# GpSimd takes over the scaling and clamping of the first six weight units, and the opening of a fused attention and feed-forward kernel is put in a new order

## The chip, the cores and the metric

The kernel runs on one core of a Trainium2 chip. The core's engines have their own instruction queues, and each works through its queue strictly in order: TensorE (PE; its weight loads are listed as PEld), VectorE (DVE), ScalarE (ACT), GpSimd (POOL) and SyncE (SP), which here only issues transfers. The metric is the device time of one execution in microseconds; the median of three runs counts.

## The reference

Attention within chunks of 64 tokens, then a feed-forward block with an ELU between two products:

```python
scores = scale * np.matmul(q_c, k_c.transpose(0, 1, 2, 4, 3))   # chunks of 64 tokens, head_dim 64
scores = scores - np.max(scores, axis=-1, keepdims=True)
attn = np.exp(scores)
attn = attn / (np.sum(attn, axis=-1, keepdims=True) + 1e-09)
out = np.matmul(attn, v_c)                                      # 8 batches, 8 heads, 576 tokens
...
h = x @ w_in                                                    # x: 4608 x 512, w_in: 512 x 2048
g = np.where(h > 0.0, h, alpha * (np.exp(np.minimum(h, 0.0)) - 1.0))
return (g @ w_out).astype(np.float32)                           # w_out: 2048 x 512
```

q, k and v arrive as 32-bit floats, the two weight matrices as 64-bit floats.

## The kernel before

**Blocks and products.** The 4608 tokens are nine blocks of 512, and a block is four tiles of 128 tokens. Every matrix product runs on numbers split into a high and a low part (`xhi`, `xlo`; `wi_hi`, `wi_lo`; `wo_hi`, `wo_lo`; `ghi`, `glo`), and is the sum of three products, high by high, high by low and low by high. In block one, `hidden(f)` makes 128 rows of the hidden layer (tile `h`) from all four tiles of x in 12 matrix products of 128x512, `elu` turns them into `e`, `ghi` and `glo`, and `second_products` adds four times three products with `w_out` to the outputs `o`. f runs from 0 to 15. Below, H0 is `hidden(0)` and S0 the second products for f = 0.

**Weights come in units.** Unit u holds 128 columns of `w_in` (rows of the hidden layer u) and 128 rows of `w_out` (for f = u - 1), as pairs of 32-bit words; unit 0 has only the first. `load_unit` loads a unit into one of three buffers `st`. `prepare_units` has two steps for each unit, both on ScalarE: the high words are multiplied by `REBIAS` (L139), and the low words are brought to a form that can be joined (L144). `merge_units` then has on VectorE a clamp of the high words (L161) and two joins that build a 32-bit float in `xf` (L168, L172); ScalarE casts that to `wi_hi` and `wo_hi` (L179). `subtract_next` makes `wi_lo` and `wo_lo` on VectorE (L185). A unit's operations on high words are 128x1024, those of unit 0 are 128x512. A buffer `st` is free for the unit after next but one when L172 has read it.

**Start.** Before block one, four tiles go through `early_attention`, in ten steps: turn q and k (PE, L270), copy them (ACT, L277), scores (PE, L248), maximum and difference (DVE, L283 to L299), exponential (ACT, L303, or eight small ones, L293, for a tile in `BY_HEAD`), sum, reciprocal and product of the probabilities (DVE, L305 to L308), turn the probabilities (PE, L315), copy (ACT, L322), times v (PE, L256), and split into `xhi` (ACT, L425) and `xlo` (DVE, L426). H0 needs `xhi` of all four tiles.

**What sets the order.** Two strings of tokens are executed one after another, and each token appends instructions to the engines' queues. In `START`, q, k, v and u with a number issue loads, a single digit is the next step of that tile, r the next step of `prepare_units`, d the next step of `merge_units`, and s a `subtract_next`. `FIRST_BLOCK` has the same letters, and H for `hidden`, e for the next of four steps of `elu`, P for second products, L4 to L7 for the loads of block two's tiles, and 4 to 7 for their next step.

Of the kernel before, what the change touches and what calls it, by code (L numbers as in the profile page):

```python
# [10 lines left out]
F32 = mybir.dt.float32  # L11
# [4 lines left out]
ALU = mybir.AluOpType  # L16
# [4 lines left out]
def kernel(  # L21
# [19 lines left out]
    nc = tc.nc  # L41

    B, H, S, D = q.shape
# [4 lines left out]
    P = 128  # L48
# [4 lines left out]
    NK = DM // P  # L53
# [4 lines left out]
    NS = (NB - PLAIN) // 2  # L58
    NG = NF // 2
    LAG = 1  # L60
    T2 = TB - P

    REBIAS = 2.0 ** -112
    LARGEST = float(np.uint32(0x0FEFFFFF).view(np.float32))
# [8 lines left out]
    at = ctx.enter_context(tc.tile_pool(name="at", bufs=1))  # L73
# [6 lines left out]
    xhi = const.tile([P, NK, TB], F32R, name="xhi")  # L80
    xlo = const.tile([P, NK, TB], F32R, name="xlo")
# [50 lines left out]
    def prepare_units():  # L132

        for u in range(NU):
            low, high, _ = units[u]

            nc.scalar.mul(out=high.bitcast(F32), in_=high.bitcast(F32), mul=REBIAS)  # L139
            prepared.add((u, "high"))  # L140
            yield

            top = low.bitcast(U16)[:, :, :, :, 1]
            nc.scalar.activation(  # L144
                out=low, in_=top, func=AF.Copy, scale=2.0 ** -13, bias=2.0 ** -14 - 0.5
            )
            prepared.add((u, "low"))
            yield

    def merge_units():  # L150


        def need(u: int, word: str):
            while (u, word) not in prepared:
                next(preparation)

        for u in range(NU):
            low, high, parts = units[u]
            highf = high.bitcast(F32)
            need(u, "high")  # L160
            nc.vector.tensor_scalar(  # L161
                out=highf, in0=highf, scalar1=LARGEST, scalar2=-LARGEST, op0=ALU.min, op1=ALU.max
            )
            yield
            need(u, "low")
            y = ybuf[u % 2].bitcast(U32).rearrange(
                "p (i a t) -> p i a t", i=2, a=4)[:, :len(parts)]
            nc.vector.scalar_tensor_tensor(  # L168
                out=y, in0=high, scalar=3, in1=low, op0=ALU.logical_shift_left, op1=ALU.bitwise_or
            )  # L170
            yield
            nc.vector.scalar_tensor_tensor(  # L172
                out=y, in0=high, scalar=0x80000000, in1=y, op0=ALU.bitwise_and, op1=ALU.bitwise_or
            )
            for i, (hi, _) in enumerate(parts):
                w = y[:, i].bitcast(F32)
                if len(hi.shape) > len(w.shape):
                    w = w.rearrange("p b (c d) -> p b c d", d=Q)
                nc.scalar.copy(out=hi, in_=w)  # L179
                merged.append((parts[i], w))  # L180
            yield
# [79 lines left out]
    def first_halves(pair_of_banks):  # L261
        return pair_of_banks[:, :, :NK * C].rearrange("p i (h t) -> p i h t", h=NK)

    def early_attention(tt: int, q_sb, k_sb, get_v, kT, at, a_pool, get_banks, put, by_head: bool):


        both = get_banks()
        for i, src in enumerate((q_sb, k_sb)):
            for hp in range(NK):
                nc.tensor.transpose(  # L270
                    out=both[:, i, hp * P:(hp + 1) * P], in_=src[:, 2 * hp:2 * hp + 2, :],
                    identity=ident,
                )
        yield
        qT = at.tile([P, NK, P], F32, name="qT")
        for i, to in enumerate((qT, kT)):
            nc.scalar.copy(out=to, in_=both[:, i, :].rearrange("p (h t) -> p h t", h=NK))  # L277
        yield
        scores = first_halves(both)
        score(scores, qT, kT)  # L280
        yield
        mx = sm.tile([P, 2, NK, 1], F32, name="mx")
        nc.vector.tensor_reduce(out=mx, in_=scores, axis=AX.X, op=ALU.max)  # L283
        a = a_pool.tile([P, H, C], F32, name="a")
        a_heads = a.rearrange("p (j h) t -> p j h t", j=2)
        z = sm.tile([P, 2, NK, 1], F32, name="z")
        if by_head:

            nc.vector.tensor_scalar_mul(mx, mx, -SCALE)
            yield  # L290
            for j in range(2):
                for h in range(NK):
                    nc.scalar.activation(  # L293
                        out=a_heads[:, j, h, :], in_=scores[:, j, h, :], func=AF.Exp, scale=SCALE,
                        bias=mx[:, j, h, :], accum_out=z[:, j, h, :],
                    )
            yield
        else:
            nc.vector.tensor_tensor(  # L299
                out=a_heads, in0=scores, in1=mx.broadcast_to([P, 2, NK, C]), op=ALU.subtract  # L300
            )
            yield
            nc.scalar.activation(out=a, in_=a, func=AF.Exp, scale=SCALE)  # L303
            yield
            nc.vector.tensor_reduce(out=z, in_=a_heads, axis=AX.X, op=ALU.add)  # L305
        nc.vector.tensor_scalar_add(z, z, 1e-9)
        nc.vector.reciprocal(z, z)
        nc.vector.tensor_tensor(  # L308
            out=a_heads, in0=a_heads, in1=z.broadcast_to([P, 2, NK, C]), op=ALU.mult
        )  # L310
        yield
        turned_ps = both[:, 0, :].rearrange("p (h t) -> p h t", h=H)
        for h in range(H):
            for half in halves:
                nc.tensor.matmul(  # L315
                    turned_ps[half, h, :], lhsT=a[half, h, :], rhs=ident[half, half],
                    start=True, stop=True,
                )
        yield

        aT = at.tile([P, NK, P], F32, name="qT").rearrange("p h (j t) -> p (h j) t", j=2)
        nc.scalar.copy(out=aT, in_=turned_ps)  # L322
        yield
        x_ps = first_halves(both)
        multiply_v(x_ps, get_v(), aT.rearrange("p h (u t) -> p u h t", u=2))
        yield
        put(tt, x_ps)
        yield
# [111 lines left out]
    def hidden(f: int):  # L440
        hi, lo = w_in_slices(f)
        h = ps_h.tile([P, TB], F32, name="h")
        if f:
            for kt in range(NK):
                three(h, hi[:, kt, :], lo[:, kt, :], xhi[:, kt, :], xlo[:, kt, :],
                      kt == 0, kt == NK - 1)
        else:
            terms = [(w, xhi, kt) for w in (hi, lo) for kt in range(NK)]
            terms += [(hi, xlo, kt) for kt in range(NK)]
            for i, (w, x, kt) in enumerate(terms):  # L450
                nc.tensor.matmul(h, lhsT=w[:, kt, :], rhs=x[:, kt, :], start=i == 0,  # L451
                                 stop=i == len(terms) - 1)
        return h
# [564 lines left out]
    def warm(n: int):  # L1018
# [7 lines left out]

    BY_HEAD = (2, 4, 5)
    START = (
        "q0 k0 q1 k1 w13 v0 0 1 0 q2 0 k2 q3 0 k3 1 1 v1 0 2 v2 1 3 0 2 2 v3 1 2 3 u0 3 1 2 u1 0 "
        "r r 1 3 1 0 3 2 2 d u2 d 1 0 r d 3 3 2 s 2 0 r d 1 d 3 r 2 3 3"  # L1030
    )
    FIRST_BLOCK = (
# [7 lines left out]
    )  # L1040
    SECOND_BLOCK = (
# [83 lines left out]
    w0 = ctx.enter_context(tc.tile_pool(name="w0", bufs=1))  # L1125
    weights.append((*w_in_tiles(w0), *w_out_tiles(w0)))
    with (
        tc.tile_pool(name="start", bufs=NTT) as start,
        tc.tile_pool(name="ps_start", bufs=NTT, space=bass.MemoryType.PSUM) as ps_start,
    ):  # L1130
# [6 lines left out]
        def start_step(item: str):  # L1137
            tt = int(item)
            if tt not in tiles:
                tiles[tt] = early_attention(  # L1140
                    tt, *[loaded[kind, tt] for kind in "qk"], lambda: loaded["v", tt],
                    start.tile([P, NK, P], F32, name="kT"), start, start,
                    lambda: start_banks() if tt else warmed[0],
                    split_first_x, tt in BY_HEAD)
            next(tiles[tt])

        for item in START.split():
# [64 lines left out]
    run, f, early_tiles = (0, o_tiles(), None), -1, {}  # L1212
# [732 lines left out]
```

## Time and profile before

| | |
|---|---|
| median of three runs | 825.47 us (822.76 to 828.17) |
| the profiled execution, its own time | 825.15 us |
| its span | 823.4 us |
| PE busy | 804.4 us, 98% of the span |
| DVE busy | 613.1 us, 74% |
| ACT busy | 523.5 us, 64% |
| POOL busy | 171.1 us, 21% |

All rows of a profile below are of that one execution: start in microseconds from the start of the span, duration, engine, line of the kernel, operation, output and inputs, and in brackets the idle time before it and what ended it. Durations overlap a little, since an engine starts the next instruction before the last one has fully drained.

### The profile page before, as it was taken

How to read it: one execution, taken by the hardware profiler on the slowest of the kernel's cores; microseconds unless marked ns; L12 is line 12 of the kernel's file. 1: busy time of each engine (PE TensorE's matmuls, PEld its weight loads, DVE VectorE, ACT ScalarE, POOL GpSimd, SP SyncE). 2: the span in 40 equal slices, each digit the busy share in tenths (PEclk: the TensorE clock that was granted, in tenths of full speed). 3: DMA queues.
4: the chain of work that ended last, by engine and by line, in shares of the span. 5: the costliest groups of instructions: out<-in, count | busy, mean ns of one | idle time of the engine just before them, and what ended most of it. 6: DMA issues, size and time to landing. Idle time of an engine off the chain costs nothing.

```text
span 823.4 us, 15851 instructions
## 1 busy us (share of the span) xinstructions
PE 804.4 (98%) x5853; PEld 655.6 (80%) x5853; DVE 613.1 (74%) x914; ACT 523.5 (64%) x990; POOL 171.1 (21%) x149
## 2 busy tenths in 40 slices
PE   6799999999999999999999999999999999999997
PEld 5688878888778878878888888778788888888885
DVE  4999997666776659767656867868889956557964
ACT  5999885544554546766666445888867737776451
POOL 0000014264525531443111254000020100000100
PEclk9999999999999999999999999999999999999999
DMA  9976994889778887689986789999876585566755
GB/s 234 272 212 209 270 328 130 244 243 267 219 215 231 231 269 205 202 241 281 283 235 188 218 246 299 286 322 287 249 204 206 195 269 193 193 196 190 226 186 149
DMA packets 183229, 191.90 MB, mean 233 GB/s; under 512 B 84720, under 2 KB 151792, under 8 KB 183152
## 3 DMA queue, kind: packets, MB, share of 16 engines
q1 hardware_dynamic: 182512, 188.80, 77.2%
q0 software_dynamic: 640, 2.10, 0.6%
q8 instruction: 46, 0.75, 0.4%
q14 instruction: 31, 0.25, 0.1%
HBM read 144.18 MB, written 42.99 MB: 227 GB/s over the span
## 4 chain that ended last, share of the span: by engine, by line
PE 83%; DMA 8%; SPq 3%; ACT 2%; DVE 2%; issue 1%; DVEq 0%; ACTq 0%
PE o L434 43%; PE h L434 34%; DMA ring<-a_dram 3%; PE ps_a L248 2%; PE ps_a L256 2%; SPq L206 2%; PE h L451 1%; DMA st<-in_moe_w_out_dram 1%; DMA kept<-in_k_dram 1%; DMA a_dram<-wi_lo 1%; DMA kept<-in_q_dram 1%; DMA a_dram<-wi_hi 1%; DMA v_sb<-in_v_dram 1%; PE ps_a L315 1%; DMA ring<-w_dram 1%
## 5 line engine op out<-in xcount | busy, mean ns | idle before, releaser
L434 PE MATMUL o<-wo_hi,ghi 128*128 128x512 f32 x272 | 107.6, 396 | 0.0
L434 PE MATMUL o<-wo_hi,glo 128*128 128x512 f32 x272 | 106.1, 390 | 0.3 <-DVE glo L479 0.3
L434 PE MATMUL o<-wo_lo,ghi 128*128 128x512 f32 x272 | 106.0, 390 | 0.0
L434 PE MATMUL h<-xhi,wi_hi 128*128 128x512 f32 x228 | 84.0, 397 | 0.1
L434 PE MATMUL h<-xlo,wi_hi 128*128 128x512 f32 x228 | 82.3, 390 | 0.0
L434 PE MATMUL h<-xhi,wi_lo 128*128 128x512 f32 x180 | 70.3, 390 | 0.0
L434 PEld LDWEIGHTS o<-wo_hi,glo 128*128 128x128 f32 x272 | 51.1, 188 | 11.7 <-DVE glo L479 0.7
L434 PEld LDWEIGHTS o<-wo_hi,ghi 128*128 128x128 f32 x272 | 51.0, 188 | 11.1
L434 PEld LDWEIGHTS o<-wo_lo,ghi 128*128 128x128 f32 x272 | 51.1, 188 | 10.2
L510 POOL TENSOR_TENSOR kept<-wi_hi,wi_lo 128x512 f32<-128x512 f32 x16 | 21.7, 1376 | 158.8 <-DVE xf L172 118.2
L471 DVE SCALAR_TENSOR_TENSOR e<-e,h 128x512 f32<-128x512 f32 x48 | 32.8, 684 | 25.2 <-ACT e L469 24.8
L434 PE MATMUL o<-split,ring 128*128 128x512 f32 x216 | 51.0, 390 | 0.0
L434 PEld LDWEIGHTS h<-xhi,wi_hi 128*128 128x128 f32 x228 | 42.6, 188 | 9.8 <-ACT kept L785 0.8
L434 PEld LDWEIGHTS h<-xlo,wi_hi 128*128 128x128 f32 x228 | 42.8, 188 | 8.5
L434 PEld LDWEIGHTS o<-split,ring 128*128 128x128 f32 x216 | 40.5, 188 | 8.4
L393 ACT COPY unturned<-turned 128x512 f32<-128x512 f32 x28 | 17.4, 621 | 46.0 <-DVE turned L388 37.9
L468 ACT ACTIVATE e<-h 128x512 f32<-128x512 f32 x48 | 28.6, 596 | 25.0 <-PE h L434 22.5
L476 ACT CAST ghi<-e 128x512 fp32r<-128x512 f32 x48 | 29.8, 621 | 19.8 <-DVE e L471 19.6
L746 POOL TENSOR_TENSOR glo<-e,ghi 128x512 fp32r<-128x512 f32 x16 | 20.7, 1296 | 96.9 <-ACT ghi L744 96.9
L434 PE MATMUL h<-split,ring 128*128 128x512 f32 x168 | 40.3, 391 | 0.0
L1492 ACT ACTIVATE e<-e 128x512 f32<-128x512 f32 x64 | 39.5, 630 | 1.0
L434 PEld LDWEIGHTS h<-xhi,wi_lo 128*128 128x128 f32 x180 | 33.8, 188 | 7.5 <-DVE wi_lo L185 0.4
(225 smaller groups left out, 2011.3 us busy)
## 6 DMA issues: line engine op xcount, KB each, us to landing
ring<-a_dram SPq DMA_DIRECT2D x56, 512.0 KB, 5.3
ring<-w_dram SPq DMA_DIRECT2D x56, 512.0 KB, 4.3
wi_hi<-a_dram SPq DMA_DIRECT2D x56, 256.0 KB, 5.3
kept<-in_q_dram SPq DMA_DIRECT2D x100, 128.0 KB, 3.8
kept<-in_k_dram SPq DMA_DIRECT2D x100, 128.0 KB, 4.0
wo_lo<-lo_dram SPq DMA_DIRECT2D x20, 512.0 KB, 5.8
v_sb<-in_v_dram SPq DMA_DIRECT2D x32, 256.0 KB, 5.4
st<-in_moe_w_in_dram SPq DMA_DIRECT2D x16, 512.0 KB, 4.9
```

What stands on the lines that cost most here:

```text
L206: nc.sync.dma_start(out=dst[p0:p0 + n], in_=src[b, :, s0:s0 + n, :].rearrange("h s d -> s h d"))
L248: nc.tensor.matmul(scores[halves[c], j, hp, :], lhsT=qT[halves[j], hp, halves[c]], rhs=kT[halves[j], hp, halves[c]], start=True, stop=True,)
L256: nc.tensor.matmul(x_ps[halves[j], c, hp, :], lhsT=v_sb[halves[c], 2 * hp + j, :], rhs=aT[halves[c], :, j * NK + hp], start=True, stop=True,)
L315: nc.tensor.matmul(turned_ps[half, h, :], lhsT=a[half, h, :], rhs=ident[half, half], start=True, stop=True,)
L393: nc.scalar.copy(out=unturned, in_=turned)
L434: nc.tensor.matmul(ps, lhsT=a, rhs=b, start=start, stop=stop, skip_group_check=onto)
L468: nc.scalar.activation(out=e, in_=h, func=AF.Relu, scale=-1.0)
L471: nc.vector.scalar_tensor_tensor(out=e, in0=e, scalar=-1.0, in1=h, op0=ALU.add, op1=ALU.max)
L476: nc.scalar.copy(out=ghi, in_=e)
L510: nc.gpsimd.tensor_tensor(out=out, in0=a, in1=b, op=op)
L746: engine.tensor_tensor(out=lo, in0=e, in1=hi.bitcast(F32), op=ALU.subtract)
L1492: nc.scalar.activation(out=units[u], in_=units[u], func=AF.Exp, scale=-1.0)
```

## The change

Four edits. For units 0 to 5 (`NPOOL = 6`), scaling and clamping of the high words leave ScalarE and VectorE, and two instructions on GpSimd take their place (multiply and minimum, then maximum). For tile 1 the product of the probabilities with the reciprocal sums moves from VectorE to GpSimd. `hidden` adds its terms for f up to 2 with the high weights first (high by high, high weights by low x, then low weights). And `START` and the beginning of `FIRST_BLOCK` are in a new order, with GpSimd's queue in the order of the program.

```diff
+    NPOOL = 6
...
-            nc.scalar.mul(out=high.bitcast(F32), in_=high.bitcast(F32), mul=REBIAS)
+            highf = high.bitcast(F32)
+            if u < NPOOL:
+                nc.gpsimd.tensor_scalar(
+                    out=highf, in0=highf, scalar1=REBIAS, scalar2=LARGEST, op0=ALU.mult, op1=ALU.min)
+                nc.gpsimd.tensor_scalar(
+                    out=highf, in0=highf, scalar1=-LARGEST, scalar2=None, op0=ALU.max)
+            else:
+                nc.scalar.mul(out=highf, in_=highf, mul=REBIAS)
...
-            nc.vector.tensor_scalar(
-                out=highf, in0=highf, scalar1=LARGEST, scalar2=-LARGEST, op0=ALU.min, op1=ALU.max
-            )
-            yield
+            if u >= NPOOL:
+                nc.vector.tensor_scalar(
+                    out=highf, in0=highf, scalar1=LARGEST, scalar2=-LARGEST, op0=ALU.min, op1=ALU.max
+                )
+            if u > 3:
+                yield
...
-        nc.vector.tensor_tensor(
+        (nc.gpsimd if normal_on_pool else nc.vector).tensor_tensor(
             out=a_heads, in0=a_heads, in1=z.broadcast_to([P, 2, NK, C]), op=ALU.mult
...
-        if f:
+        if f > 2:
...
-            terms = [(w, xhi, kt) for w in (hi, lo) for kt in range(NK)]
-            terms += [(hi, xlo, kt) for kt in range(NK)]
+            terms = [(hi, x, kt) for x in (xhi, xlo) for kt in range(NK)]
+            terms += [(lo, xhi, kt) for kt in range(NK)]
...
     START = (
-        "q0 k0 q1 k1 w13 v0 0 1 0 q2 0 k2 q3 0 k3 1 1 v1 0 2 v2 1 3 0 2 2 v3 1 2 3 u0 3 1 2 u1 0 "
...
+        "q0 k0 q1 k1 w13 v0 0 1 0 q2 0 k2 q3 0 k3 v1 1 1 0 1 2 v2 1 3 2 3 0 2 2 3 u0 u1 1 2 3 v3 0 "
...
```

**ScalarE's queue in the start**, from the exponentials of tile 2 (L293 before, L303 after) to the first operations of block one. `qT` written by L322 (L332 after) is the copy of the turned probabilities, `st` a weight unit. Before:

```order
L293 ACTIVATE a,z<-ps_a,mx 128x64 x8
L139 ACTIVATE st<-st 128x512
L144 ACTIVATE st<-st 128x512
L322 COPY qT<-ps_a 128x512 x2
L303 ACTIVATE a<-a 128x512
L139 ACTIVATE st<-st 128x1024
L179 CAST wi_hi<-xf 128x512
L322 COPY qT<-ps_a 128x512
L425 CAST xhi<-ps_a 128x2x4x64
L144 ACTIVATE st<-st 128x1024
L425 CAST xhi<-ps_a 128x2x4x64
L322 COPY qT<-ps_a 128x512
```

After:

```order
L303 ACTIVATE a,z<-ps_a,mx 128x64 x8
L332 COPY qT<-ps_a 128x512
L313 ACTIVATE a<-a 128x512
L149 ACTIVATE st<-st 128x512
L332 COPY qT<-ps_a 128x512 x2
L435 CAST xhi<-ps_a 128x2x4x64
L332 COPY qT<-ps_a 128x512
L435 CAST xhi<-ps_a 128x2x4x64 x2
L188 CAST wi_hi<-xf 128x512
L435 CAST xhi<-ps_a 128x2x4x64
L149 ACTIVATE st<-st 128x1024 x2
```

The scalings of units 0 to 2 (L139) are gone, tile 3's exponential stands ahead of unit 0's low words, and all four `xhi` stand ahead of the low words of units 1 and 2.

**GpSimd's queue after the identity matrix is made.** L318 is the product for tile 1, L139 and L141 are the two new instructions of a unit (units 0, 1, 2 here; those of 3, 4 and 5 follow in the same way). Before, the next row after the identity was a sum of block two. After:

```order
masks.py:199 AFFINE_SELECT ident<-ident 128x128
L318 TENSOR_TENSOR a<-a,z 128x512
L139 TENSOR_SCALAR st<-st 128x512
L141 TENSOR_SCALAR st<-st 128x512
L139 TENSOR_SCALAR st<-st 128x1024
L141 TENSOR_SCALAR st<-st 128x1024
L139 TENSOR_SCALAR st<-st 128x1024
L141 TENSOR_SCALAR st<-st 128x1024
```

Twelve instructions of this kind and one product are added to this queue, and nothing stood there before.

**VectorE's queue at the beginning of block one**, from unit 1's `wi_lo`, or the clamp ahead of it, to f = 0's `glo`. Before:

```order
L161 TENSOR_SCALAR st<-st 128x1024
L185 TENSOR_TENSOR wi_lo<-xf,wi_hi 128x512
L168 SCALAR_TENSOR_TENSOR xf<-st 128x1024
L471 SCALAR_TENSOR_TENSOR e<-e,h 128x512
L185 TENSOR_TENSOR wo_lo<-xf,wo_hi 128x4x4x32
L172 SCALAR_TENSOR_TENSOR xf<-st,xf 128x1024
L479 TENSOR_TENSOR glo<-e,ghi 128x512
L161 TENSOR_SCALAR st<-st 128x1024
L185 TENSOR_TENSOR wi_lo<-xf,wi_hi 128x512
```

After:

```order
L194 TENSOR_TENSOR wi_lo<-xf,wi_hi 128x512
L175 SCALAR_TENSOR_TENSOR xf<-st 128x1024
L481 SCALAR_TENSOR_TENSOR e<-e,h 128x512
L194 TENSOR_TENSOR wo_lo<-xf,wo_hi 128x4x4x32
L179 SCALAR_TENSOR_TENSOR xf<-st,xf 128x1024
L489 TENSOR_TENSOR glo<-e,ghi 128x512
L194 TENSOR_TENSOR wi_lo<-xf,wi_hi 128x512
```

The clamps (L161) are gone, and the rest stands in the same order. SyncE's queue has v of tile 3 behind units 0 and 1 instead of ahead of them, and the loads of tile 4 ahead of unit 3 instead of behind it.

More of the change, by code (lines that the diff above doesn't have):

```diff
@@ L174, in merge_units @@
             )
+            if not u:
+                yield
             for i, (hi, _) in enumerate(parts):
@@ L262, in first_halves, with early_attention @@
         return pair_of_banks[:, :, :NK * C].rearrange("p i (h t) -> p i h t", h=NK)
-    def early_attention(tt: int, q_sb, k_sb, get_v, kT, at, a_pool, get_banks, put, by_head: bool):
+    def early_attention(tt: int, q_sb, k_sb, get_v, kT, at, a_pool, get_banks, put, by_head: bool,
+                        normal_on_pool: bool = False):
         both = get_banks()
@@ L1028 @@
     START = (
-        "q0 k0 q1 k1 w13 v0 0 1 0 q2 0 k2 q3 0 k3 1 1 v1 0 2 v2 1 3 0 2 2 v3 1 2 3 u0 3 1 2 u1 0 "
-        "r r 1 3 1 0 3 2 2 d u2 d 1 0 r d 3 3 2 s 2 0 r d 1 d 3 r 2 3 3"
+        "q0 k0 q1 k1 w13 v0 0 1 0 q2 0 k2 q3 0 k3 v1 1 1 0 1 2 v2 1 3 2 3 0 2 2 3 u0 u1 1 2 3 v3 0 "
+        "r 0 3 1 r 2 1 r u2 2 2 3 3 0 1 2 d d 0 3 1 3 3 d 2 s r r r"
     )
     FIRST_BLOCK = (
[7 rows of a table removed]
[7 rows of a table added]
     )
@@ L1127 @@
     with (
+        tc.manual_schedule(engines={mybir.EngineType.Pool}),
         tc.tile_pool(name="start", bufs=NTT) as start,
@@ L1143, in start_step @@
                     lambda: start_banks() if tt else warmed[0],
-                    split_first_x, tt in BY_HEAD)
+                    split_first_x, tt in BY_HEAD, tt == 1)
             next(tiles[tt])
```

14 rows, old and new, of the table FIRST_BLOCK are left out of this document.

## The prediction

> **What bounds the kernel.** I read the busy times first, then the 40 slices, then the chain of waits in order of time.
>
> ```profile
> PE 804.4 (98%) x5853; PEld 655.6 (80%) x5853; DVE 613.1 (74%) x914; ACT 523.5 (64%) x990; POOL 171.1 (21%) x149
> PE   6799999999999999999999999999999999999997
> DVE  4999997666776659767656867868889956557964
> sum 30.00, PE 18.75 PEld 16.14 DVE 17.94 ACT 19.71 POOL 0.70; mean PE 1.25 PEld 1.08 DVE 1.20 ACT 1.31 POOL 0.05
> 30.00:100.00 70.00, 70.00 (x571) 56.42 (x570) 66.85 (x94) 64.50 (x124) 0.00 (x0) 1.00 0.78 235
> 28.89 3.02 PE h L451 x12
> 31.91 0.87 PE ps_a L270 x8
> 32.78 2.73 PE h L434 x12
> 45.60 2.95 PE h L434 x12
> ```
>
> TensorE is the bound: 98% of the span. The slices (20.6 us each) show idle time only in the first two and the last. The sum over the first 30 us has PE at 18.75. In the row of the stretch 30 to 100, the columns after its length are the busy times of PE, PEld, DVE, ACT and POOL: PE 70.00 of 70.00 us, DVE 66.85, ACT 64.50, POOL none. The chain rows carry the rest: H0 begins at 28.89, then comes the turn of tile 4, H1 at 32.78, and H3 at 45.60, and PE never waits in between. So there are two ways to move the end: start H0 earlier than 28.89, or make PE wait after it. What PE loses there it does not get back, as it is full. VectorE, 95% busy in this stretch, has little left to give.
>
> **Start.** What ends last before H0 is ScalarE:
>
> ```profile
> 13.52 0.66 PE L270 MATMUL ps_a<-ident,k_sb 128*128 128x128 f32 x4 [1.63 <-DMA k_sb<-in_k_dram]
> 18.23 0.69 DVE L299 TENSOR_TENSOR a<-ps_a,mx 128x512 f32<-128x512 f32 x1
> 20.69 0.64 ACT L303 ACTIVATE a<-a 128x512 f32<-128x512 f32 x1
> 21.74 0.69 DVE L305 TENSOR_REDUCE z<-a 128x8 f32<-128x512 f32 x1
> 22.19 1.11 ACT L139 ACTIVATE st<-st 128x1024 f32<-128x1024 f32 x1 [0.86 <-DMA st<-in_moe_w_out_dram]
> 22.91 0.69 DVE L308 TENSOR_TENSOR a<-a,z 128x512 f32<-128x512 f32 x1
> 23.74 1.21 PE L315 MATMUL ps_a<-ident,a 64*64 64x64 f32 x31 [1.56 <-DVE a L308]
> 26.86 0.69 PE L256 MATMUL ps_a<-qT,v_sb 64*64 64x64 f32 x32 [1.37 <-ACT qT L322]
> 27.77 1.06 ACT L425 CAST xhi<-ps_a 128x512 fp32r<-128x512 f32 x2
> 28.89 1.20 PE L451 MATMUL h<-xhi,wi_hi 128*128 128x512 f32 x4 [1.34 <-ACT xhi L425]
> ```
>
> The last k lands at 13.5, and the loads up to it don't change, so all before that stays. Behind it:
> - VectorE loses tile 1's product (0.6 of its queue), so tile 3's difference starts at 17.6 instead of 18.23 and ends at 18.3. Tile 3's exponential (20.69) no longer stands behind unit 0's two operations and a second copy; behind one copy (0.5) it runs from 18.9 to 19.5.
> - Its sum, reciprocals and product took from 21.74 to 23.60. From 19.55 they end at 21.4, the turn (1.2) at 22.6 instead of 24.95.
> - Times v for tiles 0 to 2 takes 0.62 each, as the row's 0.69 less the overlap, and tile 3's last copy stands behind one `xhi`: tile 3's times v ends at 25.0 instead of 27.55. Then tile 3's `xhi`, unit 0's `wi_hi` and tile 2's `xhi` at some 0.5 each: H0 at **26.6**, 2.3 earlier.
>
> Tile 1's product on GpSimd (1.3, the row of `glo` below) ends at 18.0, ahead of the PE step that needs it. Unit 0's two GpSimd steps end before 21, and its joins have until 25.6. v of tile 3 moves behind units 0 and 1; three transfers of 512 KB later it lands near 22, and it is needed at 24.4: nothing.
>
> **The first wait.** H1 needs unit 1's `wi_hi`. VectorE first does tile 2's `xlo` and unit 0's `wi_lo` (0.6 each from 26.6), then unit 1's joins (1.22 each), then ScalarE casts (0.6), with some 0.05 from each to the next: 31.1. PE is ready for it at 26.6 + 3.02 + 0.87 = 30.5. H1 at 31.1 instead of 32.78: of the 2.3 there are 1.7 left, and VectorE reaches unit 1's `wi_lo` at some 31.2, only about 0.2 to 0.3 ahead of the 31.49 of the profile. From here VectorE decides.
>
> **Block one, where the change costs.** VectorE and GpSimd block each other:
>
> ```profile
> 119.54 1.30 POOL L510 TENSOR_TENSOR kept<-wi_hi,wi_lo 128x512 f32<-128x512 f32 x1 [118.23 <-DVE xf L172]
> 120.09 1.29 DVE L185 TENSOR_TENSOR wi_lo<-xf,wi_hi 128x512 fp32r<-128x512 f32 x1
> 123.38 0.68 DVE L185 TENSOR_TENSOR wo_lo<-xf,wo_hi 128x512 fp32r<-128x512 f32 x1
> ...
> 130.36 0.69 DVE L479 TENSOR_TENSOR glo<-e,ghi 128x512 fp32r<-128x512 f32 x1
> 130.51 0.58 POOL L1248 COPY kept<-xlo 128x1 f32<-128x1 f32 x1 [8.54 <-DVE xlo L1184]
> ```
>
> The subtraction that met a running GpSimd instruction took 1.29 instead of 0.68, and ended 0.54 after that one: it stood still until GpSimd was done. The other way round, a GpSimd copy of one column, with a single input, took 0.58 and ended with VectorE's `glo`. So L168, L172, L185 and L479, which all read two tiles, don't run beside GpSimd. Clamps are removed, but two GpSimd instructions for each unit are put in the way.
>
> Their price isn't in the trace. The nearest rows:
>
> ```profile
> 0.34 0.10 POOL L1930 MEMSET const-uint8-127<- 128x1 uint8 x1
> 0.73 0.20 POOL masks.py:197 MEMSET ident<- 128x128 f32 x1 [0.29 <-POOLq L1930]
> 1.01 0.29 POOL masks.py:199 TENSOR_SCALAR_AFFINE_SELECT ident<-ident 128x128 f32<-128x128 f32 x1
> L479 POOL TENSOR_TENSOR glo<-e,ghi 128x512 fp32r<-128x512 f32 x13 | 16.8, 1292 | 33.4 <-ACT ghi L476 33.4
> L597 POOL TENSOR_TENSOR g_kept<-g_kept 128x1024 fp32r<-128x1024 f32 x2 | 4.8, 2403 | 0.0
> ```
>
> Less 0.10, writing alone goes at 0.8 ns a column (0.10 for 128), the select, which reads one tile, at 1.5, and two inputs come to 2.40 for 128x1024. So one 128x1024 instruction with one input lies between 0.9 and 2.4; the select's rate gives 1.6. I take **1.2**, between the two rows with one input or none, since the select also makes its condition.
>
> [...]
>
> When they run: a unit's load waits for the buffer that its third predecessor leaves.
>
> ```profile
> 21.91 0.37 SPq L118 DMA_DIRECT2D st<-in_moe_w_in_dram  x1
> 30.88 0.37 SPq L118 DMA_DIRECT2D st<-in_moe_w_in_dram  x1
> 36.03 0.87 SPq L118 DMA_DIRECT2D st<-in_moe_w_in_dram  x1
> st<-in_moe_w_in_dram SPq DMA_DIRECT2D x16, 512.0 KB, 4.9
> ```
>
> Units 3, 4 and 5 are issued at 21.91, 30.88 and 36.03 and land some 5 to 7 later; after the change unit 3 goes out some 3 later, behind its slower joins, the other two near those times. So units 1 and 2 (landed by 25) are handled mostly while VectorE waits for `xhi`, but the six instructions of units 3 to 5 fall into 31 to 47, where VectorE is full:
>
> ```profile
> 30.72 0.69 DVE L161 TENSOR_SCALAR st<-st 128x1024 f32<-128x1024 f32 x1
> 31.49 0.69 DVE L185 TENSOR_TENSOR wi_lo<-xf,wi_hi 128x512 fp32r<-128x512 f32 x1
> 35.64 0.68 DVE L479 TENSOR_TENSOR glo<-e,ghi 128x512 fp32r<-128x512 f32 x1
> 36.24 0.69 DVE L161 TENSOR_SCALAR st<-st 128x1024 f32<-128x1024 f32 x1
> 36.84 0.69 DVE L185 TENSOR_TENSOR wi_lo<-xf,wi_hi 128x512 fp32r<-128x512 f32 x1
> 44.01 0.68 DVE L185 TENSOR_TENSOR wi_lo<-xf,wi_hi 128x512 fp32r<-128x512 f32 x1
> ```
>
> From unit 1's `wi_lo` (31.49) to unit 3's (44.01) VectorE works without a gap. Of its clamps only unit 3's (36.24) lies there, worth 36.84 - 36.24 = 0.6; the others come before or after. Against that, six GpSimd instructions, each of which holds up a two-input instruction nearly for its whole length (the first ones find VectorE in one with a PSUM input now and then: 95%).
>
> **The sum.** Unit 3's `wi_lo`: -0.2 (start) - 0.6 (clamp) + 6 x 1.2 x 0.95 = 6.8, so 6.0 later. Before, it ended at 44.69, and H3 needs it at its third product, 45.60 + 0.46: 1.4 to spare. H3 is 6.0 - 1.4 = **4.6 later**. After that no GpSimd instruction of a unit is left, the clamps of units 4 and 5 are gone too, so PE loses no more and regains nothing. ScalarE loses 6 scalings (1.1 each), which is worth nothing while VectorE decides. The new term order of H1 and H2 lets PE start before `wi_lo`, which doesn't help as glo of the same f holds S0 and S1; inside the sum, nothing.
>
> The profiled execution's own time is 825.15 (span 823.4), 0.3 under the median; 825.15 + 4.6 = 829.8. With 0.9 an instruction the six cost 5.1 and the end is 2.9 later, 828.1; with 1.6 it is 9.1 - 2.2 = 6.9, 832.1; with 2.4 it is 11.5, 836.6.
>
> **Rivals.**
> - *GpSimd's work falls into gaps.* The six land where VectorE does sums, maxima or `e`, or waits. For it: this trace has single GpSimd instructions without harm; against it: 66.85 of 70 us busy. Then S0 decides: `glo` comes 4.15 after unit 1's `wi_lo`, as from 31.49 to 35.64, at 35.3, done at 36.0, against 36.6 for the third product of S0 now: 0.7 earlier, **824.4**. If the profile's spare time covers the H1 wait as well, the whole 2.3 stays, 822.8.
> - *GpSimd's price is that of two inputs, or the strided words slow it.* From about 1.8 an instruction (6 x 1.8 x 0.95 = 10.3, less 2.2) the end is more than 8 later, and at 2.4 units 1 and 2 also reach into the joins that H1 waits for: 834 to **838**, slower by over 1%.
> - *It doesn't reach the start at all*, because v of tile 3 lands after 24.4 or GpSimd's product holds tile 1: H0 stays near 28.9, and the blocks come on top of the same queue: 831, within the forecast's own range.
>
> **Chances.** A measurement of this kernel tells about 1% from no change: 817.2 and 833.7 around the median. The forecast (827 to 833) has 0.50, gaps (822 to 826.5) 0.35, the dear GpSimd (834 to 838) 0.12, a start that gains nothing 0.02, and something faster by over 1% 0.01, since only 11 us of idle PE lie in the first 30. The range 822.5 to 834.5 leaves out the dear case and little else. Faster 0.01, within 1% 0.86, slower 0.13.
>
> **What the new profile would show.** H0 near 26.6; a wait ahead of H1 on unit 1's `wi_hi`; VectorE subtractions and joins of 1.5 to 2.4 us where GpSimd runs between 31 and 47; GpSimd instructions of 1.2 for 128x1024; PE waits of together some 6 to 7 between 30 and 55, on `glo` and `wi_lo`. I am wrong if PE shows no waits there, if the GpSimd rows are far from 1.2, or if VectorE's rows keep their 0.69 and 1.22.

## The result and the profile after

The changed kernel takes **834.45 us** (median of six runs, 831.98 to 836.46), beside 825.37 (822.76 to 828.17) for the kernel before in six runs of the same chip: ratio 1.0106, 95% interval 1.0080 to 1.0133. The profiled execution took 832.64 with a span of 830.9, so 7.5 more than the 823.4 of before. The forecast was 829.8 with a range of 822.5 to 834.5; the time lies 0.05 inside the upper end, and where the rival of a dear GpSimd had put it (834 to 838).

The page of the changed kernel, its busy times, two rows of its slices and the first row of its chain, and then the two stretches that were shown of before. The columns after the length are again PE, PEld, DVE, ACT, POOL, granted clock, DMA share and GB/s:

```profile
PE 806.4 (97%) x5853; PEld 656.8 (79%) x5853; DVE 616.3 (74%) x907; ACT 518.3 (62%) x984; POOL 213.6 (26%) x162
PE   6689999999999999999999999999999999999997
POOL 2980004165515632344111264100020010000100
PE 84%; DMA 4%; DVE 4%; ACT 3%; POOL 2%; SPq 2%; issue 1%; ACTq 0%; DVEq 0%; POOLq 0%
```

```profile
0.00:30.00 30.00, 21.38 (x449) 18.41 (x449) 18.39 (x31) 17.14 (x40) 14.65 (x12) 1.00 0.94 249
30.00:100.00 70.00, 62.14 (x493) 49.10 (x492) 62.27 (x81) 54.07 (x108) 28.56 (x8) 0.98 0.66 207
```

In the first 30 us TensorE does 2.6 us more (21.38 against 18.75): the start is earlier, though not all of that comes from the new order (see the timeline below). From 30 to 100 it does 7.9 us less (62.14 of 70): it waits, and GpSimd, which did nothing there before, is busy for 28.56 us and now stands in the chain that ended last: from 16.75 to 35.75 that chain goes through GpSimd's rows. So TensorE is idle 5.2 us longer up to 100 us. Its busy time over the whole span is 2.0 longer (806.4 against 804.4) for the same 5853 products. That is 7.2 of the 7.5.

Where it waits, in the timeline of PE (idle time and releaser in brackets; the first row is the turn of the last k of the start, and `wi_lo` at 61.05 belongs to H4):

```profile
12.06 0.66 PE L280 MATMUL ps_a<-ident,k_sb 128*128 128x128 f32 x4 [0.25 <-DMA k_sb<-in_k_dram]
26.27 1.20 PE L461 MATMUL h<-xhi,wi_hi 128*128 128x512 f32 x4 [1.70 <-ACT xhi L435]
31.84 1.20 PE L461 MATMUL h<-xhi,wi_hi 128*128 128x512 f32 x4 [1.68 <-ACT wi_hi L188]
38.30 0.50 PE L444 MATMUL o<-wo_hi,ghi 128*128 128x512 f32 x1 [2.81 <-ACT ghi L486]
40.30 0.73 PE L444 MATMUL o<-wo_hi,glo 128*128 128x512 f32 x1 [1.23 <-DVE glo L489]
44.28 1.09 PE L461 MATMUL h<-xhi,wi_hi 128*128 128x512 f32 x4
50.57 1.15 PE L325 MATMUL ps_a<-ident,a 64*64 64x64 f32 x32 [0.65 <-DVE a L318]
61.05 0.50 PE L444 MATMUL h<-xhi,wi_lo 128*128 128x512 f32 x1 [1.46 <-DVE wi_lo L194]
```

H0 starts at 26.27, H1 at 31.84, H2 at 44.28 (38.9 before). The turn of the last k began at 12.06 in this execution and at 13.52 in that of before, with the same loads ahead of it; so 1.5 of the 2.6 us by which H0 is earlier come from ahead of the first step that the change touches. Between and behind H0 and H1 come waits that were not there. Their source is two steps back, in the timelines of POOL (L139 multiply and minimum, L141 maximum; units 1 to 3, and the last row of unit 5), VectorE and ScalarE:

```profile
20.51 4.31 POOL L139 TENSOR_SCALAR st<-st 128x1024 f32<-128x1024 f32 x1
24.90 2.92 POOL L141 TENSOR_SCALAR st<-st 128x1024 f32<-128x1024 f32 x1
27.90 4.84 POOL L139 TENSOR_SCALAR st<-st 128x1024 f32<-128x1024 f32 x1
32.83 2.91 POOL L141 TENSOR_SCALAR st<-st 128x1024 f32<-128x1024 f32 x1
35.82 4.84 POOL L139 TENSOR_SCALAR st<-st 128x1024 f32<-128x1024 f32 x1
...
56.15 2.98 POOL L141 TENSOR_SCALAR st<-st 128x1024 f32<-128x1024 f32 x1
```

```profile
27.86 1.23 DVE L175 SCALAR_TENSOR_TENSOR xf<-st 128x1024 uint32<-128x1024 uint32 x1 [0.32 <-POOL st L141]
29.12 2.02 DVE L179 SCALAR_TENSOR_TENSOR xf<-st,xf 128x1024 uint32<-128x1024 uint32 x1
35.77 1.23 DVE L175 SCALAR_TENSOR_TENSOR xf<-st 128x1024 uint32<-128x1024 uint32 x1 [3.26 <-POOL st L141]
36.92 0.68 DVE L481 SCALAR_TENSOR_TENSOR e<-e,h 128x512 f32<-128x512 f32 x1
37.63 0.62 ACT L486 CAST ghi<-e 128x512 fp32r<-128x512 f32 x1 [3.20 <-DVE e L481]
```

A unit costs GpSimd 7.2 to 7.9 us instead of the 2.4 of the forecast, and its rows follow one another without a gap until 59.1. Unit 2 is done at 35.74. VectorE's join of unit 2 (L175) stands in its queue ahead of `e` of H0 (L481), so VectorE sits idle for 3.26 us, ScalarE for 3.20 ahead of `ghi`, and TensorE for 2.81 ahead of S0. Behind this wait the granted clock (the third number from the end) drops:

```profile
40.00:42.00 2.00, 1.70 (x4) 1.43 (x5) 1.92 (x3) 2.00 (x4) 1.92 (x2) 0.60 0.49 135
42.00:44.00 2.00, 2.00 (x6) 1.54 (x6) 1.97 (x5) 1.01 (x3) 1.92 (x2) 0.55 0.97 377
```

At 0.60 and 0.55 the products of S0 follow one another every 0.43 us, against 0.23 at 1.00 in the kernel before. The ten of them from 40.30 to 44.28 take 3.98 us; at the pace of before (twelve from 36.07 to 38.92) they would by this estimate take some 2.4, so the drop costs some 1.6 us, which is most of the 2.0 us of longer busy time. PE waited 2.81 and then 1.23 us ahead of the drop. With the order alone (first experiment below) the clock fell to 0.50 from 40 to 42 behind waits of 0.65 and 0.74 us, so what sets off a drop stays open.

### The profile page after: what moved, and what is told of

It is laid out like the page before. It is cut to its first block, busy times and chain, and to the rows that moved or that the text cites. A ratio compares the mean times of both kernels' runs of the same rounds, so it can differ in the third digit from the quotient of the medians.

```text
span 830.9 us, 15864 instructions
## 1 busy us (share of the span) xinstructions
PE 806.4 (97%) x5853; PEld 656.8 (79%) x5853; DVE 616.3 (74%) x907; ACT 518.3 (62%) x984; POOL 213.6 (26%) x162
## 4 chain that ended last, share of the span: by engine, by line
PE 84%; DMA 4%; DVE 4%; ACT 3%; POOL 2%; SPq 2%; issue 1%; ACTq 0%; DVEq 0%; POOLq 0%
PE o L444 45%; PE h L444 33%; PE ps_a L257 2%; PE h L461 2%; PE ps_a L265 2%; POOL st L139 1%; SPq L215 1%; DMA ring<-a_dram 1%; DVE xf L175 1%; POOL st L141 1%; DMA st<-in_moe_w_out_dram 1%; DVE xf L179 1%; DMA st<-in_moe_w_in_dram 1%; DMA lo_dram<-wo_lo 1%; ACT st L149 1%
## 5 line engine op out<-in xcount | busy, mean ns | idle before, releaser
L444 PE MATMUL h<-xhi,wi_hi 128*128 128x512 f32 x204 | 74.4, 396 | 0.1
L444 PE MATMUL h<-xlo,wi_hi 128*128 128x512 f32 x204 | 73.0, 390 | 0.0
L444 PE MATMUL h<-xhi,wi_lo 128*128 128x512 f32 x156 | 61.1, 392 | 1.5 <-DVE wi_lo L194 1.5
L481 DVE SCALAR_TENSOR_TENSOR e<-e,h 128x512 f32<-128x512 f32 x48 | 32.8, 683 | 25.5 <-ACT e L479 25.2
L444 PEld LDWEIGHTS h<-xhi,wi_hi 128*128 128x128 f32 x204 | 38.2, 188 | 8.8 <-ACT kept L795 0.7
L444 PEld LDWEIGHTS h<-xlo,wi_hi 128*128 128x128 f32 x204 | 38.4, 188 | 7.6
L489 DVE TENSOR_TENSOR glo<-e,ghi 128x512 fp32r<-128x512 f32 x35 | 29.2, 835 | 12.3 <-ACT ghi L486 11.9
```

The lines of the kernel that those rows point to most:

```text
L444: nc.tensor.matmul(ps, lhsT=a, rhs=b, start=start, stop=stop, skip_group_check=onto)
L481: nc.vector.scalar_tensor_tensor(out=e, in0=e, scalar=-1.0, in1=h, op0=ALU.add, op1=ALU.max)
L489: engine.tensor_tensor(out=glo, in0=e, in1=ghi.bitcast(F32), op=ALU.subtract)
```

## Experiments

The theory at first was that VectorE waits for GpSimd's **late results**. The rivals: GpSimd **holds VectorE up** while it works (the forecast's theory, "port" in some of the expectations; the runs show whether and for how long, but not by what means), and the **order** by itself costs. Each ratio is against the kernel before, measured beside it on the same chip (its median there: 826.6 to 827.6 us; 1% is some 8.3 us), with its 95% interval.

**The order alone.** Everything of the change but GpSimd's work on the units; scalings and clamps are back on ScalarE and VectorE.

```diff
-    NPOOL = 6
+    NPOOL = 0
```

> The new order without the weights on GpSimd: ScalarE scales and VectorE clamps all units again, in the places where the new order has them; GpSimd keeps only tile 1's product. [...] If the new order itself costs, 830 or more stays.

Measured: 829.59 us, ratio 1.0040 (1.0020 to 1.0059). With the units back on ScalarE and VectorE the loss is smaller than in the changed kernel (1.0106), but it is not gone: the order is not good by itself. The turn of the last k, H0 and H1:

```profile
13.85 0.66 PE L280 MATMUL ps_a<-ident,k_sb 128*128 128x128 f32 x4 [1.14 <-DMA k_sb<-in_k_dram]
28.24 1.19 PE L461 MATMUL h<-xhi,wi_hi 128*128 128x512 f32 x4 [1.70 <-ACT xhi L435]
33.41 1.21 PE L461 MATMUL h<-xhi,wi_hi 128*128 128x512 f32 x4 [1.27 <-ACT wi_hi L188]
```

With the units back on the two engines, H0 comes at 28.24 (26.27 with GpSimd, 28.89 before). Most of that difference is the last k, whose turn began at 13.85 here, at 12.06 with GpSimd and at 13.52 before. From that turn to H0 it takes 14.39 us here, 14.21 with GpSimd and 15.37 before: the new order gains some 1.0 to 1.2 us on H0, with GpSimd's work or without it. H1 comes at 33.41, later than before, and PE waits 3.5 us between 30 and 100.

**GpSimd's work with nobody waiting for it.** The order alone, and GpSimd does the same kind of instructions on scratch memory beside it (units 0 to 4, with 768 columns in the last).

```diff
+            if u < 5:
+                scratch = xf[:, 0, :, P * (u == 4):]
+                scratch = scratch[:, :, ::2]
+                scratch = scratch[:, :(NK if u else 2)]
+                nc.gpsimd.tensor_scalar(
+                    out=scratch, in0=scratch, scalar1=REBIAS, scalar2=LARGEST, op0=ALU.mult, op1=ALU.min)
+                nc.gpsimd.tensor_scalar(
+                    out=scratch, in0=scratch, scalar1=-LARGEST, scalar2=None, op0=ALU.max)
...
+        nc.gpsimd.memset(xf[:, 0], 0.0)
```

> [...] Theory of the late results: VectorE's rows lengthen here and there, PE waits under 2 us more than in e1_order, time within 2 us of e1_order. Theory of the port, which stood in the prediction: most of the 9 us comes back, 831 or more.

Measured: 833.30, ratio 1.0079 (1.0059 to 1.0099), so some 0.4% over the order alone, where the port theory had put it (831 or more). Holding up VectorE costs something, but here the clamps are still on VectorE; the cleaner pair is below.

**The words packed.** The same with words that stand next to one another, to see whether the step of two words makes GpSimd slow.

```diff
-                scratch = scratch[:, :, ::2]
+                scratch = scratch[:, :, :(TB - P * (u == 4)) // 2]
```

> As e2_port, with the same number of columns side by side instead of every second one. If the step of two words makes the instructions dear, 128x1024 falls from 4.3 to 4.8 (multiply and minimum) and 2.9 (maximum) to 1.2 to 2.4; if it is the operation, the rows stay at 4.3 and 2.9.

Measured in one run: 834.48. The two kernels' first 128x1024 instructions, every second word, then packed:

```profile
21.87 3.96 POOL L142 TENSOR_SCALAR xf<-xf 128x1024 f32<-128x1024 f32 x1
25.91 2.94 POOL L144 TENSOR_SCALAR xf<-xf 128x1024 f32<-128x1024 f32 x1
```

```profile
21.76 3.64 POOL L142 TENSOR_SCALAR xf<-xf 128x1024 f32<-128x1024 f32 x1
25.48 2.78 POOL L144 TENSOR_SCALAR xf<-xf 128x1024 f32<-128x1024 f32 x1
```

The step costs 0.2 to 0.3 us. It is the operation that is dear: in these packed rows 2.78 us with one operation, 3.64 with two.

**H1's products twice.** The changed kernel with H1's 12 products done twice, to keep TensorE busy in the wait ahead of S0 and see what the clock does.

```diff
-            for i, (w, x, kt) in enumerate(terms):
+            for i, (w, x, kt) in [*enumerate(terms)] * (2 if f == 1 else 1):
```

> The change with the 12 products of H1 done twice into the same tile, so that PE works in the 2.8 us in which it otherwise waits ahead of S0; the result is unchanged. If the fall of the granted clock to 0.55 to 0.60 between 40 and 44 follows from that idle time, the clock stays at 1.00 there and the time is some 1.5 to 2 us under that of the change (832.5 to 833 in place of 834.45); if the clock falls anyway, or the 2.7 us of work are in the way, the time is the same or up to 2 us longer.

Measured: 841.50, ratio 1.0168 (1.0145 to 1.0192). That is 7 us over the changed kernel, outside both expectations. The clock stayed at 1.00 from 28 to 60, as wished, which fits idle time as the cause of the drop, in one execution. But the products stood ahead of tile 4's scores (39.13 instead of 34.80), and this execution was 1.4 late already at H0, so its time says nothing of the clock's price.

**Nobody scales or clamps units 0 to 5.** The changed kernel with that work left out on every engine; what it would be with a GpSimd that costs nothing.

```diff
-            if u < NPOOL:
-                nc.gpsimd.tensor_scalar(...)
-                nc.gpsimd.tensor_scalar(...)
-            else:
+            if u >= NPOOL:
                 nc.scalar.mul(out=highf, in_=highf, mul=REBIAS)
...
-                out=y, in0=high, scalar=3, in1=low, ...
+                out=y, in0=high, scalar=0 if u < NPOOL else 3, in1=low, ...
```

> The changed kernel, but nobody scales or clamps units 0 to 5 (neither GpSimd nor the two other engines; the join doesn't shift these units, so that the numbers stay finite). GpSimd does only tile 1's product. Theory 'late results' (TensorE waits in 30 to 100 us because GpSimd's chain of some 7.8 us a unit delivers late): the 7.9 us of idle TensorE between 30 and 100 us go, and with them the lower clock behind them; H0 near 26, span 830.9 - 7.9 - 2 = 821, time 822 to 824, ratio to before 0.995 to 0.998. Theory 'port' (VectorE is held up by GpSimd): the same. Rival 'order' (the new order by itself makes TensorE wait, as in the kernel with the order alone, 829.6): over 1.5 us of waits stay in 30 to 100 us, time 826 or more.

Measured: 827.46, ratio 1.0004 (0.9988 to 1.0020). The 822 to 824 of the two theories did not come; the time is that of the rival 'order', with 1.5 us of waits left (first row of the next pair).

**The same, with GpSimd's twelve instructions and no reader.** GpSimd reads the units' high words when they have landed, and writes elsewhere.

```diff
+                scratch = xf[:, 0] if u < 3 else weights[1][3][:, :4]
...
+                    out=scratch, in0=highf, scalar1=REBIAS, scalar2=LARGEST, op0=ALU.mult, op1=ALU.min)
...
+                    out=scratch, in0=scratch.bitcast(F32), scalar1=-LARGEST, scalar2=None, op0=ALU.max)
```

> As the kernel in which nobody scales units 0 to 5, but GpSimd again does its twelve instructions: it reads the units' high words when they land, and writes into memory that nobody reads. Between this and the kernel without them stands what GpSimd costs others while it works (port, buffers held); between this and the changed kernel what waiting for its results costs. Theory 'late results': within 1.5 us of the kernel without them (822 to 825.5), waits in 30 to 100 us under 2 us. Theory 'port': 4 us and more above it, 828 to 833, with VectorE's joins and subtractions beside GpSimd 0.3 to 0.9 us longer and waits of over 4 us.

Measured: 830.69, ratio 1.0047 (1.0031 to 1.0062), 3.2 us over the kernel without them. The stretch 30 to 100 of the two, without GpSimd's work and with it:

```profile
30.00:100.00 70.00, 68.53 (x560) 54.32 (x559) 64.23 (x89) 60.86 (x119) 0.00 (x0) 1.00 0.78 240
```

```profile
30.00:100.00 70.00, 66.01 (x543) 51.32 (x542) 66.05 (x86) 58.17 (x114) 28.46 (x8) 1.00 0.74 228
```

This pair splits the loss. PE waits 1.5 us in this stretch with the order and no work, 4.0 with GpSimd's work beside it, 7.9 when its results are needed. In ratios: 1.0004, 1.0047, 1.0106. So **about 0.4% is what GpSimd's work does to the others, and about 0.6% what waiting for it costs**, each to some 0.2% to 0.3%; neither theory alone. The 0.6% holds the slower clock behind the waits as well. That GpSimd holds the units' buffers is not the cause of the 0.4%: in the second kernel the loads of units 4 to 8 are issued 0.13 to 0.14 us after VectorE's second join (L182) has ended (the first of them at 31.20, after 31.07), and the GpSimd instruction that reads the same buffer has ended 2.7 us or more ahead of that. How VectorE is held up, in the second kernel's timelines of POOL and VectorE:

```profile
51.46 4.09 POOL L142 TENSOR_SCALAR wo_lo<-st 128x1024 fp32r<-128x1024 f32 x1
55.63 3.41 POOL L144 TENSOR_SCALAR wo_lo<-wo_lo 128x1024 fp32r<-128x1024 f32 x1
```

```profile
53.81 1.24 DVE L178 SCALAR_TENSOR_TENSOR xf<-st 128x1024 uint32<-128x1024 uint32 x1 [0.33 <-ACT st L152]
54.95 0.69 DVE L197 TENSOR_TENSOR wi_lo<-xf,wi_hi 128x512 fp32r<-128x512 f32 x1
56.16 2.13 DVE L182 SCALAR_TENSOR_TENSOR xf<-st,xf 128x1024 uint32<-128x1024 uint32 x1
```

Beside the first GpSimd instruction VectorE's join and subtraction take their usual 1.24 and 0.69. Beside the second one join takes 2.13, 0.9 more. In all, nine of VectorE's rows between 20 and 60 are 0.3 to 0.9 longer than in the kernel without GpSimd's work, 6.9 us together: never the 3 to 5 us for which a GpSimd instruction runs.

**The twelve instructions cut in halves.** To see whether a stall comes with each instruction or with its size.

```diff
+                for a in range(2):
                     nc.gpsimd.tensor_scalar(
-                        out=scratch, in0=highf, ...
+                        out=scratch[:, :, 2 * a:2 * a + 2], in0=highf[:, :, 2 * a:2 * a + 2], ...
```

> As the kernel in which GpSimd's twelve instructions have no reader, with each of them cut into two halves: 24 instructions on the same words. There, twelve instructions lengthened VectorE's busy time in 0 to 100 us from 80.47 (none) to 84.16 us, one row of 0.75 to 0.9 us for nearly each of them. Theory 'one stall for each instruction': twice as many, VectorE 87 to 88 us, waits of TensorE in 30 to 100 us 6 to 7 us instead of 4.0, ratio to before 1.0075 to 1.0095. Rival 'a share of the time in which GpSimd works' (which stays the same, some 40 us): VectorE 84 to 85 us, waits near 4 us, ratio 1.004 to 1.006.

Measured: 831.16, ratio 1.0038 (1.0023 to 1.0053); VectorE busy for 83.2 us up to 100. It is not one stall of the same size for each instruction: fourteen rows are now longer, but by 0.23 to 0.48 each, 5.6 us together, as here:

```profile
55.34 1.13 DVE L201 TENSOR_TENSOR wo_lo<-xf,wo_hi 128x512 fp32r<-128x512 f32 x1
56.40 1.21 DVE L186 SCALAR_TENSOR_TENSOR xf<-st,xf 128x1024 uint32<-128x1024 uint32 x1
57.53 1.13 DVE L496 TENSOR_TENSOR glo<-e,ghi 128x512 fp32r<-128x512 f32 x1
```

So the sum stays near that of the whole instructions, as the rival had it, if a little under its bounds. PE's waits in 30 to 100 are 2.1 us, but the clock was 0.56 and 0.58 from 28 to 32, so they can't be set beside the 4.0.

What the stall goes with can be read in the changed kernel, from two GpSimd instructions of 1024 columns and the rows beside them:

```profile
40.74 3.06 POOL L141 TENSOR_SCALAR st<-st 128x1024 f32<-128x1024 f32 x1
43.88 4.81 POOL L139 TENSOR_SCALAR st<-st 128x1024 f32<-128x1024 f32 x1
```

```profile
40.94 1.59 DVE L194 TENSOR_TENSOR wo_lo<-xf,wo_hi 128x512 fp32r<-128x512 f32 x1
44.98 1.59 DVE L489 TENSOR_TENSOR glo<-e,ghi 128x512 fp32r<-128x512 f32 x1
47.62 1.10 DVE L316 TENSOR_SCALAR z<-z 128x8 f32<-128x8 f32 x1
```

An instruction of 3.06 us and one of 4.81 lengthen a subtraction by the same 0.9, and halves of 512 columns by at most 0.48. So in these rows the stall goes with the columns of the GpSimd instruction and not with its duration. A row with a single input of 8 columns is held up too: L316 takes 1.10 instead of 0.17, until 0.03 us after GpSimd's instruction has ended.

**GpSimd for units 0 and 1 alone.**

```diff
-    NPOOL = 6
+    NPOOL = 2
```

> The changed kernel with GpSimd preparing units 0 and 1 alone (both end by 28 us); 2 to 5 go back to ScalarE and VectorE, the order stays the new one. Theory 'late results': the four units taken away were the late ones, so the waits of 3.3, 2.8 and 1.5 us behind GpSimd go; H0 at 26.3 and H1 at 31.8 as in the changed kernel, and what is left are waits of some 2 us as in the order alone: 826 to 828.5. Rival 'order' (the four units' work in that order is what costs): 829 to 831, no better than the order alone (829.6).

Measured: 830.34, ratio 1.0033 (1.0017 to 1.0050). That is in the range of the rival 'order' (829 to 831): better than six units, no better than none (1.0040). In the profile the waits from 30 on are small (0.75, 0.21 and 0.84 us), but this execution's clock was 0.50 to 0.94 from 20 to 32.

**One instruction for each unit.** The lower clamp of units 0 to 5 is left out.

```diff
-                nc.gpsimd.tensor_scalar(
-                    out=highf, in0=highf, scalar1=-LARGEST, scalar2=None, op0=ALU.max)
```

> The changed kernel without the second GpSimd instruction of each of the six units: the lower clamp is left out, nobody does it. A unit then takes GpSimd 4.3 to 4.8 us instead of 7.2 to 7.9. Theory 'late results': most of the waits behind GpSimd go; of TensorE's 7.9 us of waits in 30 to 100 us 2.5 to 4 are left (1.5 that the order has without any GpSimd work, half of the 2.5 that GpSimd's work adds without a reader, and what is still late), ratio to before 1.002 to 1.006. Rival 'any wait of VectorE and ScalarE behind GpSimd costs, however long the chain': waits of 6 us or more, ratio 1.0075 or more.

Measured: 829.23, ratio 1.0022 (1.0000 to 1.0044).

```profile
30.00:100.00 70.00, 66.65 (x545) 52.57 (x544) 62.94 (x85) 57.18 (x112) 11.98 (x3) 0.98 0.70 215
```

```profile
32.65 3.80 POOL L139 TENSOR_SCALAR st<-st 128x1024 f32<-128x1024 f32 x1 [4.26 <-ACT wo_hi L186]
36.64 4.19 POOL L139 TENSOR_SCALAR st<-st 128x1024 f32<-128x1024 f32 x1 [0.19 <-DMA st<-in_moe_w_out_dram]
43.83 3.99 POOL L139 TENSOR_SCALAR st<-st 128x1024 f32<-128x1024 f32 x1 [3.00 <-DMA st<-in_moe_w_out_dram]
```

As "late results" had it: waits of 3.35 us. At some 4 us a unit GpSimd is idle ahead of units 3 and 5 (4.26 and 3.00 us); at 7.2 to 7.9 it never is, and the others wait for it. The loss does not grow with the price in proportion: with no work on GpSimd the ratio is 1.0004, with one instruction a unit 1.0022, with two 1.0106.

**`elu` ahead of the waiting joins.** The changed kernel with `FIRST_BLOCK` in a new order at three places, so that S0 no longer stands behind the join of unit 2.

```diff
-H d L4 d s 4 u3 r e d e 4 s e d e s H ... 4 e e d P e H L5 ... d e r d d s e r s u7 d e u8 d P
+H d L4 d s 4 u3 r e e 4 s e e d d s H ... 4 e e e d P H L5 ... d e r s e s e d d r u7 d u8 d P
```

> The changed kernel, in which no step of elu and no subtraction stands behind a join that waits for GpSimd any more: all of H0's elu goes ahead of unit 2's joins, H1's glo ahead of unit 3's first join, and unit 4's two subtractions and H3's glo ahead of unit 5's joins. GpSimd's work and its price stay. Theory 'queue' (GpSimd's results are late, but what TensorE waits for is the work that stands behind the waiting join in VectorE's queue): the waits of 2.81 and 1.23 us ahead of S0 and of 1.46 us in H4 go, TensorE's waits in 30 to 100 us fall from 7.9 to 3.5 to 5.5 us, the ratio to before is 1.0045 to 1.0075, near the 1.0047 that GpSimd's work costs without a reader. Rival 'chain' (H2 to H5 need weights that come at the pace of GpSimd's 7.2 to 7.9 us a unit, whatever the queue's order): the wait moves ahead of H2, H4 or H5, the waits stay at 7 us or more and the ratio at 1.009 to 1.012.

Measured: 836.63, ratio 1.0135 (1.0108 to 1.0162). This other order of VectorE's queue doesn't win the loss back. PE's rows:

```profile
40.83 1.20 PE L461 MATMUL h<-xhi,wi_hi 128*128 128x512 f32 x4 [1.32 <-ACT wi_hi L188]
44.92 0.50 PE L444 MATMUL o<-wo_hi,ghi 128*128 128x512 f32 x1 [1.05 <-ACT ghi L486]
51.12 1.15 PE L325 MATMUL ps_a<-ident,a 64*64 64x64 f32 x32 [2.91 <-DVE a L318]
```

H2 starts at 40.83, 3.4 earlier than in the changed kernel (44.28), but it waits for unit 2's weights, and tile 4's turn, whose input stands behind unit 3's joins (GpSimd is done with unit 3 at 44.9), now waits 2.91 instead of 0.65. What gets past one late unit meets the next, and PE waits 8.7 us in 30 to 100, as "chain" had it. Why the ratio came out above its 1.009 to 1.012 is not settled; in this execution the clock was lower in the first 30 us (0.94), and H0 was 1.3 later than in the changed kernel's, 1.1 of it from the last k (turn at 13.20).

**Old order of block one, new start, units 0 and 1 on GpSimd.** A version that might keep the gain of the start.

```diff
-    NPOOL = 6
+    NPOOL = 2
...
-            if u > 3:
+            if u:
                 yield
...
-        "r 0 3 1 r 2 1 r u2 2 2 3 3 0 1 2 d d 0 3 1 3 3 d 2 s r r r"
+        "r 0 3 1 r 2 1 r u2 2 2 3 3 0 1 2 d d 0 3 1 3 3 d 2 s r r d d"
...
     FIRST_BLOCK = (        # as before the change
```

> Old order of block one, new order of the first four tiles, units 0 and 1 on GpSimd, tile 1's product on GpSimd, high weights first in H0 to H2. If the loss is in the new block one and its GpSimd work: H0 at 26.3 instead of 28.9, H1 at 31.8 instead of 32.8, no wait in 35 to 100 us, span 823.4 - 0.9 = 822.5, time 823.5 to 825.5, ratio 0.997 to 1.000. Rival: the gain of the start is not passed on, because H1's weights come no earlier (H1 at 33 or later): 826 to 829.

Measured: 827.53, ratio 1.0015 (0.9997 to 1.0032). No gain. In the profiled execution, the fastest of the twelve (824.77), H0 came at 26.91, but then:

```profile
30.85 1.40 PE L280 MATMUL ps_a<-ident,io 128*128 128x128 f32 x8 [0.93 <-DMA io<-in_q_dram]
36.76 0.50 PE L444 MATMUL o<-wo_hi,glo 128*128 128x512 f32 x1 [0.44 <-DVE glo L489]
```

Tile 4's load is late for the earlier start, and then `glo`: the next thing in line takes back 1.4 of the 2.0 us, of which 0.9 were an earlier last k (12.67). No version tried beat the kernel before.

## Why the forecast missed by 4.6 us, step by step

- **TensorE as the bound, and that a wait after H0 is not made good:** held. 7.2 of the 7.5 us are its idle time up to 100 us and its longer busy time, most of which is the slower clock behind the waits.
- **Start:** half of it held, and luck did the rest. H0 came at 26.27 (forecast 26.6), but the forecast let the last k land at 13.5 as before, and its turn began at 12.06. In the other executions with the new order it began at up to 13.85, so this is no doing of the change. From that turn to H0 the new order won 1.2 us (14.21 against 15.37), not 2.3. With the k of before, the 7.5 us between the two profiled executions would by this estimate be some 9, and the medians are 9.1 apart. H1 waits for unit 1's `wi_hi` as foretold, at 31.84 (31.1). The 0.7 between is unit 1's second join, 2.02 instead of 1.22, held up by GpSimd.
- **Price of a GpSimd instruction: the step that failed.** 1.2 was taken, with 0.9 and 2.4 as bounds; measured were 2.9 to 3.1 with one operation and 4.3 to 4.8 with two, beyond both. The rows used as neighbours (a memset, a select of 128 columns, a product of two tiles) did not bound it, and the two instructions were priced alike though one has two operations.
- **That an instruction holds up VectorE "nearly for its whole length": failed the other way.** It was read off one pair of rows, in which both instructions had two inputs. Here an instruction of 3 to 4.8 us lengthens such a row by at most 0.93 (1.62 instead of 0.69 for `wo_lo` at 52.87 with `elu` ahead of the joins), mostly 0.3 to 0.9. That a row with a PSUM input is not held up, as the 95% took it, agrees with `e`: it reads `h` from PSUM, and took 0.67 to 0.69 beside GpSimd's instructions in the changed kernel. With the true price and the forecast's 95%, the six instructions of units 3 to 5 would have cost over 20 us; the two errors partly cancelled, so it is luck that the forecast loss of 4.6 us was nearer than its parts, and that the time still fell inside the range. Held up, all in all: some 0.4%, 3.6 us.
- **Waiting for the result was not in the sum.** At the forecast's 2.4 us a unit there was nothing to wait for; at 7.2 to 7.9 the units follow one another without a gap from 16.75 to 59.1, and TensorE waits behind their joins at S0 and in H4. That is some 0.6%. The rival of a dear GpSimd had the time, and of the price the direction (1.8 to 2.4, still too low); of its two reasons, strided words cost only 0.2 to 0.3, and products with two inputs are cheaper here (1.04 for 128x512 against 1.57 and 2.02). Of the late results it had only that units 1 and 2 would reach into the joins for H1.
- **The rival in which GpSimd fits into gaps (824.4):** it did not come even with GpSimd's work gone altogether: the new order then takes 1.0004 times the time before, though the interval (0.9988 to 1.0020) would still allow its 0.999. The gain of the start is not passed on: in that kernel waits of 0.49 ahead of H1, 0.46 on `glo` and 0.46 on `wi_lo` come in its place.
- **The clock** was in no step. Nine of the eleven other profiles with the new start showed a lower clock somewhere between 14 and 56 us (0.50 at 16 to 18 and at 40 to 42 with the order alone, 0.55 and 0.60 at 28 to 32 with GpSimd's work on scratch, 0.50 at 22 to 24 with two units). That of before showed none there, nor did those of the pair that splits the loss. How much of the ratio it makes over many executions stays open.

The measured 1.06% sits on the bound of what the forecast took a measurement to tell, 1%: its interval, 0.8% to 1.3%, allows both "within 1%" and "slower".

## What to carry to other kernels

Before work is moved to another engine, price the very instruction there, with its number of operations; neighbours of another kind don't bound it. Then ask two things of the new owner apart: how much it disturbs others while it works, and when its last result is due against when it comes, counted as a chain from the first unit on. An early start is worth only what the next loads and results let through: look for what is second in line before counting it. And before a gain at the start is read off two profiles, count both from the last event that the change cannot have moved, as here from the last k.

## What was not expected of the hardware

- GpSimd's multiply and minimum of 128x1024 takes 3.6 to 4.1 us packed and 3.8 to 4.8 with every second word; its maximum alone 2.8 to 3.4 and 2.9 to 4.1; 128x512 takes 2.0 and 1.6. VectorE does both clamps of such a tile in 0.69.
- A running GpSimd instruction with one input of 1024 columns lengthened a VectorE row with two inputs by at most 0.93 us (1.62 instead of 0.69), whether it ran for 3.06 or 4.81, and one of 512 columns by at most 0.48.
- The turn of the last k began anywhere between 12.06 and 13.85 us in twelve executions with the same loads ahead of it.
